# Empty slots in the side stream of a spectral and MLP kernel, row blocks loaded in two halves, and the filter gradient reordered on ScalarE

## The chip, the cores and the metric

The kernel runs on one core of a Trainium2 chip. The metric is the device time of one execution in microseconds (us). TensorE is called PE here, VectorE DVE, ScalarE ACT, GpSimdE POOL and SyncE SP. DMAs are issued from the queues of SP, POOL and, for one kind of load, ACT.

## The reference

The reference is the forward pass and all gradients of a gated mixture of two branches on an input x of 2048 x 1024 (bfloat16):

```
g = sigmoid(sum(x * gate_w))                      # one gate for each row
a = irfft2(rfft2(x) * (w_r + i w_i))              # spectral filter, w of 2048 x 513
h = relu(x @ w1 + b1) ** 2                        # 2048 x 3584
b = h @ w2 + b2
out = g * a + (1 - g) * b
```

Given grad_out, it returns out (out_0) and the gradients of x (out_1), w_r and w_i (out_2 and out_3), w1 (out_4), b1 (out_5), w2 (out_6), b2 (out_7) and gate_w (out_8).

## The kernel before

The program is unrolled completely. Its large products (five times 896 matmuls of 128x512, and a last one that is cut into fewer products) are the main stream of PE. The two-dimensional transforms of x and of the gradient are a side stream of small matmuls that is strewn among them. Both are Python generators: a `yield` is the end of a unit of work, and `spread` (a few lines above the program's end) takes from the side generator as many units as are due after each unit of the main one. A unit with nothing in it, a bare `yield`, is an empty slot.

A planner of the framework fixes the order of each engine's instructions when the program is built. It goes through a simulated time, and gives an engine that is free the instruction that comes first in program order among those that it holds to be ready by then. Program order thus decides only where several instructions are ready. An engine with nothing else to do takes work from far ahead: four loads of w2 (L554) that stand behind the first eight tiles of a stage are issued together at its start. At run time each engine and each DMA queue keeps its fixed order, and where the planner was too hopeful the engine waits, with all that is queued behind.

The stages in order:

- Up to about 446 us: `mlp_in` makes h and its gradient dh for all of the 3584 hidden columns (L667 and L677), stores both (h2T_scr, dhT_scr), and the first half of the transforms of x and grad_out (row tiles, columns) lies among them and goes to z_scr.
- 446 to about 890 us: `mlp_grads` makes the gradients of w2 (L808) and w1 (L824). A main unit is 16 matmuls of 128x512 into one PSUM bank (pw, two banks in turn), which ACT copies out (wo, L812 and L829); there are 112 of them. The side stream is `spectra`, which is `fft_mid` and then `fft_out`. Two main units run first. Then `todo / 110` side units are due after each main unit, with `todo = 3 + 6 * 16 + 2 * 16 = 131`, the number of side units that are to be done by the end.
- 890 to about 1101 us: `mlp_out` makes the forward output (L896) with w2 in SBUF and row blocks of h2T_scr (tile hblk, `blocks.one`, L844: 3584 rows by 256 columns, 1792 KB, two buffers). The second half of `fft_out` lies among it.
- From 1101 us on: `GradOfX` makes the gradient of x from row blocks of dhT_scr (hblk again) and the transposed w1, with a scheme of seven products on quarters of the block: a11 and a21 are the columns 0 to 127 and 128 to 255 of the first half of the 28 row chunks, a12 and a22 those of the second half. DVE makes the sums of quarters (dS L984, dT L991) and adds the products (L1005), in an order that the program chains by hand (`dve`).

The side stream in more detail. `fft_mid` loads am and bm (L308, L310), the first z and wn (L316, L320), and in `edges` the first column of all z (ed, low, mid, L341 to L343), from which PE makes 32 small products (sp, L354). Then, for m from 0 to 15, six units: `transform` twice (px L375, copied to x by ACT, L377), the first product of the inverse of m - 1 (`back`, pv L411), `products` (t, L383 and L385, on DVE) with the second one, `joined` (y, L392 and L393), and a unit with `grads_of_w` and `mirrored` for the next m (pm, L368 and L369, which the next transform reads). The end of `back` makes two tiny products (si, L424) and stores to y_scr (L435). In m = 0 there is no `back`, so it has four units.

`grads_of_w` (L441 to L453) multiplies on DVE into g1 and g2, adds in two pieces for each of the two gradients into gs with the 512 columns written in another order (L446, with the last column in L447), scales by a constant into gw (L449), scales the first and last column once more from gs (L450) and stores gw with four DMAs of POOL's queue.

`fft_out` loads ki and ci, and two row tiles r of y_scr (L505, ACT's queue), which need all that `fft_mid` stored there. Then it has two units for each of 32 tiles: `rows_back` (pki L521, from r and the folded rf, L513 and L514) and `columns_back` (pui L294, folds on DVE, a store to ax_scr).

Of the kernel before, what the change touches and what calls it, by code (L numbers as in the profile page):

```python
# [10 lines left out]
P = 128  # L11
# [3 lines left out]
ALU = mybir.AluOpType  # L15
ACT = mybir.ActivationFunctionType

FDT = FP16
# [3 lines left out]
def pair_of(m, R1):  # L22
    return (m, R1 - m) if m else (0, R1 // 2)
# [112 lines left out]
def kernel(  # L136
# [22 lines left out]
    nc = tc.nc  # L159
# [6 lines left out]
    g = Geo(S, D, F)  # L166
    S2, DC, FC = g.S2, g.DC, g.FC
    R1, R2 = g.R1, g.R2
    NT = S // P
    Q, H, LW, W1 = D // 4, D // 2, g.Df + 1, g.Df  # L170
# [4 lines left out]
    GS = 2.0 / (S * D * XS * XS)  # L175
    SBUF, PSUM, DRAM = bass.MemoryType.SB, bass.MemoryType.PSUM, bass.MemoryType.DRAM
    turned = lambda out, in_: nc.sync.dma_start(out=out, in_=in_, transpose=True)
    ld, st = nc.sync.dma_start, nc.gpsimd.dma_start
    V, mm = nc.vector.tensor_tensor, nc.tensor.matmul
# [10 lines left out]
    def pool(name, side="left", space=SBUF, stack=None, bufs=1):  # L190
        stack = ExitStack() if stack is None else stack
        kw = {} if space == DRAM else dict(side=side, reuse_waits="tile")
        return stack.enter_context(tc.tile_pool(name=name, bufs=bufs, space=space, **kw)), stack

    pers, _ = pool("pers", stack=ctx)
    dram, _ = pool("dram", space=DRAM, stack=ctx)
# [25 lines left out]
    def after(ins, earlier, wait=mybir.DependencyClass.Sync):  # L222

        if earlier is not None:
            info = mybir.DependencyInfo(wait, mybir.DependencyReason.DATA)
            tc.add_manual_dep(ins.ins, earlier.ins.name, info, reason="paced")
# [75 lines left out]
    def fft_mid():  # L302
        fb, fbs = pool("f2", "right")
# [8 lines left out]
        def inputs(m):  # L312
            z = fb.tile([P, 2, 2, H], FDT, name="z", tag="z", bufs=2)
            for n, c in enumerate((m, R1 // 2 + m)):
                for x in range(2):
                    ld(out=z[lanes[x], n], in_=z_scr[:][c, :, x ^ n if m else x])  # L316
            wn = fb.tile([P, 2, LW], BF16, name="wn", tag="wn", bufs=2)
            for c_, src_w in enumerate((A_w_r, A_w_i)):
                for n, k in enumerate(pair_of(m, R1)):
                    ld(out=wn[lanes[n], c_, 0:W1], in_=every(src_w, k))  # L320
            return z, wn
# [50 lines left out]
        def transform(m, n, pm, x):  # L372
            px = fps.tile([P, 2, H], FP32, name="px", tag="ps2", bufs=2)
            for T in range(2):
                mm(px[:, T, :], lhsT=am[:, m, n, :], rhs=pm[:, n, T, :], start=True, stop=True)  # L375
            for c in range(2):
                nc.scalar.copy(out=x[lanes[n], c, :, 0:H], in_=px[lanes[c]])  # L377

        def products(x, w):
            t1_ = fb.tile([P, 2, 2, LW], FDT, name="t1", tag="t1")  # L380
            t2_ = fb.tile([P, 2, 2, LW], FDT, name="t2", tag="t2")
            xw = lambda t: t[:].rearrange("p c t l -> p (c t) l")[:, :, 0:W1]
            V(out=xw(t1_), in0=xw(x), in1=w[:, 0:1, 0:W1].to_broadcast([P, 4, W1]), op=ALU.mult)  # L383
            wi = w[:, 1:3, 0:W1].rearrange("p (o t) l -> p o t l", o=1).to_broadcast([P, 2, 2, W1])
            V(out=t2_[:, :, :, 0:W1], in0=x[:, :, :, 0:W1], in1=wi, op=ALU.mult)  # L385
            return t1_, t2_
# [47 lines left out]
                for h in range(2):  # L434
                    st(out=y_scr[:][c, :, h ^ n if m else h], in_=pc[lanes[h], n])  # L435

        def grads_of_w(m, x):
            XA, XB = (x[:, :, T, 0:W1] for T in range(2))
            t1_ = fb.tile([P, 2, LW], FDT, name="g1", tag="g1")
            t2_ = fb.tile([P, 2, LW], FDT, name="g2", tag="g2")  # L440
            V(out=t1_[:, :, 0:W1], in0=XB, in1=XA, op=ALU.mult)  # L441
            V(out=t2_[:, :, 0:W1], in0=XB, in1=XA[:, ::-1, :], op=ALU.mult)
            gs = fb.tile([P, 2, LW], FDT, name="gs", tag="gs")
            for c, (a, b, op) in enumerate(((t1_[:, 0], t1_[:, 1], ALU.add), (t2_[:, 1], t2_[:, 0], ALU.subtract))):
                grouped = lambda t: t[:, 0:H].rearrange("p (g i) -> p g i", g=4)
                V(out=gs[:, c, 0:H].rearrange("p (i g) -> p g i", g=4), in0=grouped(a), in1=grouped(b), op=op)  # L446
                V(out=gs[:, c, H:W1], in0=a[:, H:W1], in1=b[:, H:W1], op=op)  # L447
            gw = fb.tile([P, 2, LW], BF16, name="gw", tag="gw")
            nc.vector.tensor_scalar(out=gw[:, :, 0:W1], in0=gs[:, :, 0:W1], scalar1=GS, scalar2=None, op0=ALU.mult)  # L449
            nc.vector.tensor_scalar(out=gw[:, :, 0::H], in0=gs[:, :, 0::H], scalar1=0.5 * GS, scalar2=None, op0=ALU.mult)  # L450
            for c_, dst_w in enumerate((out_2, out_3)):
                for n, k in enumerate(pair_of(m, R1)):
                    st(out=every(dst_w, k), in_=gw[lanes[n], c_, 0:W1])  # L453
# [2 lines left out]
        ex = edges()  # L456
        pm, w = mirrored(0, nxt[0]), by_groups(nxt[1])
        nxt = inputs(1)
        held = None
        yield  # L460
        for m in range(NM + 1):
            if m < NM:
                x = fb.tile([P, 2, 2, LW], FDT, name="x", tag="x", bufs=2)
                for n in range(2):
                    transform(m, n, pm, x)
                    yield
                nc.vector.tensor_copy(out=x[:, :, :, 0::H], in_=ex[:, m])
            if held:
                backs = back(m - 1, *held)
                next(backs)  # L470
                yield
            if m < NM:
                ts = products(x, w)
            if held:
                next(backs)
                yield
                for _ in backs:
                    pass
            if m < NM:
                held = joined(m, *ts)  # L480
                yield
                grads_of_w(m, x)
                if m + 1 < NM:
                    pm, w = mirrored(m + 1, nxt[0]), by_groups(nxt[1])
                if m + 2 < NM:
                    nxt = inputs(m + 2)
                yield
        fbs.close()

    def fft_out():  # L490
# [3 lines left out]
        fb, fbs = pool("f3", "right")  # L494
# [59 lines left out]
                    ld(out=w2[:, fc : fc + 4, :], in_=B_w2[fc * P : (fc + 4) * P, :].rearrange("(q p) e -> p q e", p=P))  # L554

        load(0), load(1)
        yield
        yield
        folded(0)
        for n in range(len(tiles) + 1):  # L560
            if n < len(tiles):
# [275 lines left out]
    BW = 2 * P  # L837

    def blocks(scr):
        v_ = scr[:].rearrange("c p s -> p c s")  # L840

        def one(k, earlier=None):
            t_ = later["strm"].tile([P, FC, BW], BF16, name="hblk", tag="strm", bufs=2)
            after(ld(out=t_[:], in_=v_[:, :, k * BW : (k + 1) * BW]), earlier)  # L844
            return t_

        return one
# [326 lines left out]
    for k in range(NT // 4):  # L1174
        i = 4 * k
# [38 lines left out]
    n = 0  # L1214
# [22 lines left out]
    def spectra():  # L1237
        yield from fft_mid()
        yield from fft_out()

    spec, grads = spectra(), mlp_grads()
    next(grads), next(grads)
    todo = 3 + 6 * (R1 // 2) + 2 * NT
    for _ in spread(grads, spec, todo / (2.0 * FG * FGC * NH - 2)):
        pass
    tps_s.close()
    out_, n = mlp_out(), 0
# [44 lines left out]
```

## Time and profile before

| what | before |
|---|---|
| median of 3 runs | 1285.03 us (1284.2 to 1285.09) |
| the profiled execution | 1284.05 us, span 1282.3 us |
| mean granted clock of PE | 0.995 |
| PE busy | 1259.7 us |
| DVE, ACT, POOL busy | 737.9, 474.1, 275.7 us |
| gs adds, L446 and L447 | 32 x 1304 ns and 32 x 277 ns (DVE) |
| gw scaling, L449 and L450 | 16 x 429 ns and 16 x 237 ns (DVE) |
| row blocks hblk | 16 loads of 1792 KB, 8.1 to 10.6 us to landing |
| r from y_scr | 32 loads of 256 KB, 2.7 to 9.7 us to landing, median 4.9 |

How to read it: the span is the time from the first to the last instruction of one profiled execution. Busy times of engines overlap. A group's line gives the source line, the engine, the operation, what it writes and reads, the count, and then the total and the mean of one. A wait names the instruction that waited and the one that released it. A granted clock below 1.00 means that PE ran slower than it can in that stretch: at 0.50 a matmul of 128x512 takes twice as long.

### The profile page before, as it was taken

Reading aid. Unit: us, or ns where it says so; the run is one execution under the profiler, and the core shown is the slowest. Engines: PE = TensorE matmul, PEld = TensorE weight load, DVE = VectorE, ACT = ScalarE, POOL = GpSimd, SP = SyncE. Lnnn points to the kernel's source line nnn. Section 1 sums busy time; section 2 is a strip of 40 time slices with the busy share of each in tenths; the row PEclk is TensorE's granted clock in tenths of the full one; section 3 lists DMA queues with packets and bytes.
Section 4 is the critical chain, followed back from the end, with each engine's and each line's share of the span. In section 5 each row is a group of like instructions: output and inputs, shape, how many; then the busy total and the mean of one; then the engine's idle time right before and its main releaser. Section 6 shows DMA issues by size and latency. Waiting matters only on the chain.

```text
span 1282.3 us, 18371 instructions
## 1 busy us (share of the span) xinstructions
PE 1259.7 (98%) x6884; PEld 610.6 (48%) x6884; DVE 737.9 (58%) x1634; ACT 474.1 (37%) x777; POOL 275.7 (22%) x424
## 2 busy tenths in 40 slices
PE   9999999999999999999999999999999999999997
PEld 5555544555544444444444444555455454444443
DVE  3554433544482237687787772343867767886573
ACT  4656654666633324434433432443112111011100
POOL 0111111111100135445465542222010101000000
PEclk9999999999999999999999999999999999999999
DMA  9566353546344678998879669965899897565530
GB/s 290 201 181 181 132 156 124 180 149 189 107 133 119 149 196 222 237 254 186 197 181 182 165 141 289 272 194 170 223 231 220 192 208 206 163 183 162 166 114 33
DMA packets 326004, 233.27 MB, mean 182 GB/s; under 512 B 195052, under 2 KB 279178, under 8 KB 325658
## 3 DMA queue, kind: packets, MB, share of 16 engines
q1 hardware_dynamic: 290864, 141.19, 46.4%
q0 software_dynamic: 26144, 82.47, 18.9%
q10 hardware_dynamic: 8906, 8.43, 2.3%
q8 instruction: 54, 0.88, 0.3%
q14 instruction: 36, 0.29, 0.1%
HBM read 106.19 MB, written 81.81 MB: 147 GB/s over the span
## 4 chain that ended last, share of the span: by engine, by line
PE 57%; DVE 4%; issue 1%; DMA 0%; ACT 0%; ACTq 0%; DVEq 0%
PE pw L824 15%; PE acc L896 14%; PE pw L808 13%; PE xX L996 7%; PE xV L996 4%; PE xZ L996 1%; PE pui L294 1%; PE pki L521 1%; PE pv L411 1%; PE px L375 1%; DVE dT L991 1%; DMA r<-y_scr 0%; DVE dS L984 0%; DVE af L876 0%; DVE g L963 0%
## 5 line engine op out<-in xcount | busy, mean ns | idle before, releaser
L667 PE MATMUL ph<-xT,w1g 128*128 128x512 bf16 x896 | 221.1, 379 | 1.0 <-DMA w1g<-in_B_w_dram 1.0
L677 PE MATMUL pd<-dbT,w2T 128*128 128x512 bf16 x896 | 211.3, 379 | 0.4 <-DVE dhT L681 0.4
L824 PE MATMUL pw<-grp,res 128*128 128x512 bf16 x896 | 203.2, 381 | 0.0
L808 PE MATMUL pw<-dbn,grp 128*128 128x512 bf16 x896 | 203.0, 383 | 0.0
L896 PE MATMUL acc<-w,hblk 128*128 128x512 bf16 x896 | 198.7, 379 | 0.0
L681 DVE SCALAR_TENSOR_TENSOR dhT<-pd,rT 128x512 bf16<-128x512 f32 x112 | 77.4, 691 | 203.0 <-PE pd L677 162.9
L808 PEld LDWEIGHTS <-grp 128*128 128x128 bf16 x896 | 87.4, 99 | 105.9 <-issue 4.8
L677 PEld LDWEIGHTS <-w2T 128*128 128x128 bf16 x896 | 87.1, 98 | 103.4 <-issue 1.2
L824 PEld LDWEIGHTS <-res 128*128 128x128 bf16 x896 | 86.5, 98 | 99.5 <-issue 2.3
L896 PEld LDWEIGHTS <-hblk 128*128 128x128 bf16 x896 | 86.2, 98 | 98.0
L667 PEld LDWEIGHTS <-w1g 128*128 128x128 bf16 x896 | 84.6, 98 | 90.2 <-DMA w1g<-in_B_w_dram 1.3
L669 ACT ACTIVATE rT<-ph,b1col 128x512 bf16<-128x512 f32 x112 | 77.0, 687 | 115.7 <-PE ph L667 115.7
L829 ACT CAST wo<-pw 128x512 bf16<-128x512 f32 x56 | 32.8, 585 | 131.2 <-PE pw L824 74.1
L812 ACT CAST wo<-pw 128x512 bf16<-128x512 f32 x56 | 32.8, 585 | 128.4 <-PE pw L808 87.9
L962 ACT ACTIVATE g<-gatew_bc,dsc 128x1024 f32<-128x1024 bf16 x16 | 18.3, 1148 | 149.3 <-DVE gxo L1005 123.0
L670 ACT ACTIVATE h2T<-rT 128x512 bf16<-128x512 bf16 x112 | 70.6, 630 | 2.5
L996 PEld LDWEIGHTS <-dS 128*128 128x128 f16 x448 | 43.8, 98 | 52.9
L523 ACT CAST rt<-pki 128x1024 f16<-128x1024 f32 x32 | 32.5, 1016 | 96.4 <-PE pki L521 92.9
L377 ACT CAST x<-px 64x1024 f16<-64x1024 f32 x64 | 64.4, 1007 | 6.9 <-PE px L375 6.2
L283 POOL DMA_DIRECT2D z_scr<-u x32 | 22.7, 710 | 171.6 <-ACT u L278 101.7
L722 POOL DMA_DIRECT2D h2T_scr<-h2T x28 | 19.9, 711 | 183.1 <-ACT h2T L670 167.4
L897 DVE SCALAR_TENSOR_TENSOR ot<-acc,omg,af 128x512 bf16<-128x512 f32 x32 | 24.0, 748 | 52.0 <-PE acc L896 51.9
(188 smaller groups left out, 1613.2 us busy)
## 6 DMA issues: line engine op xcount, KB each, us to landing
h2T_scr<-h2T POOLq DMA_DIRECT2D x28, 512.0 KB, 4.2
dhT_scr<-dhT POOLq DMA_DIRECT2D x28, 512.0 KB, 4.6
hblk<-h2T_scr SPq DMA_DIRECT2D x8, 1792.0 KB, 9.9
hblk<-dhT_scr SPq DMA_DIRECT2D x8, 1792.0 KB, 9.3
z_scr<-u POOLq DMA_DIRECT2D x32, 256.0 KB, 3.0
z<-z_scr SPq DMA_DIRECT2D x64, 128.0 KB, 3.6
y_scr<-pc POOLq DMA_DIRECT2D x64, 128.0 KB, 3.8
r<-y_scr ACTq DMA_DIRECT2D x32, 256.0 KB, 4.9
```

What stands on the lines that cost most here:

```text
L377: nc.scalar.copy(out=x[lanes[n], c, :, 0:H], in_=px[lanes[c]])
L667: mm(ph[:], lhsT=w1g[:, dc, fc % 2 * P : (fc % 2 + 1) * P], rhs=xT[:, dc, ss], start=(dc == 0), stop=(dc == DC - 1))
L669: nc.scalar.activation(rT[:], ph[:], ACT.Relu, bias=b1col[:, fc : fc + 1])
L670: nc.scalar.activation(h2T, rT[:], ACT.Square)
L677: mm(pd[:], lhsT=w_[:, ec, fc % FGC * P : (fc % FGC + 1) * P], rhs=dbT[:, ec, ss], start=(ec == 0), stop=(ec == DC - 1),)
L681: return STT(out=dhT, in0=pd[:], scalar=2.0, in1=rT[:], op0=ALU.mult, op1=ALU.mult, accum_out=gb1part[:, fc, sb : sb + 1],)
L808: mm(pw[:], lhsT=cur[:, t, fb_ * P : (fb_ + 1) * P], rhs=dbn[:, t, hf * H : (hf + 1) * H], start=(t == 0), stop=(t == NT - 1),)
L812: last = nc.scalar.copy(out=wo[:, hf * H : (hf + 1) * H], in_=pw[:])
L824: mm(pw[:], lhsT=xr[t][:, d_ * P : (d_ + 1) * P], rhs=cur[:, t, :], start=(t == 0), stop=(t == NT - 1),)
L829: nc.scalar.copy(out=wo[:], in_=pw[:])
L896: turn["PE"] = mm(acc[:], lhsT=cur[:, fc, t2 * P : (t2 + 1) * P], rhs=w2[:, fc, cs], start=(fc == 0), stop=(fc == FC - 1))
L996: mm(acc[:], lhsT=lhs[:, fc, :], rhs=rhs[:, fc, :], start=start and fc == 0, stop=fc == KH - 1, skip_group_check=True,)
```

## The change

- `fft_mid` gives three slots instead of one after its loads and edge products, and three instead of one at the end of m = 0.
- `fft_out` gives four empty slots instead of two after its first loads.
- `todo` is 137 instead of 131, so the six slots are counted: the side stream stands at the same place when `mlp_grads` ends.
- `grads_of_w` adds without reordering, in one piece for each gradient (513 columns), into gs, which has two buffers now. A new function, `grads_out`, scales and reorders with one multiply of ACT, scales the first and last column on DVE from gs as before, and issues the four stores. It stands behind the first transform of the next m, and for the last m behind the end of `back`.
- Every row block hblk is loaded with two DMAs of 14 row chunks each, for both uses (h2T_scr and dhT_scr).

```diff
-        def grads_of_w(m, x):
+        def grads_of_w(x):
...
-            gs = fb.tile([P, 2, LW], FDT, name="gs", tag="gs")
-            for c, (a, b, op) in enumerate(((t1_[:, 0], t1_[:, 1], ALU.add), (t2_[:, 1], t2_[:, 0], ALU.subtract))):
-                grouped = lambda t: t[:, 0:H].rearrange("p (g i) -> p g i", g=4)
-                V(out=gs[:, c, 0:H].rearrange("p (i g) -> p g i", g=4), in0=grouped(a), in1=grouped(b), op=op)
-                V(out=gs[:, c, H:W1], in0=a[:, H:W1], in1=b[:, H:W1], op=op)
+            gs = fb.tile([P, 2, LW], FDT, name="gs", tag="gs", bufs=2)
+            V(out=gs[:, 0, 0:W1], in0=t1_[:, 0, 0:W1], in1=t1_[:, 1, 0:W1], op=ALU.add)
+            V(out=gs[:, 1, 0:W1], in0=t2_[:, 1, 0:W1], in1=t2_[:, 0, 0:W1], op=ALU.subtract)
+            return gs
+
+        def grads_out(m, gs):
             gw = fb.tile([P, 2, LW], BF16, name="gw", tag="gw")
-            nc.vector.tensor_scalar(out=gw[:, :, 0:W1], in0=gs[:, :, 0:W1], scalar1=GS, scalar2=None, op0=ALU.mult)
+            nc.scalar.mul(
+                out=gw[:, :, 0:H].rearrange("p c (i g) -> p c i g", g=4),
+                in_=gs[:, :, 0:H].rearrange("p c (g i) -> p c i g", g=4), mul=GS,
+            )
             nc.vector.tensor_scalar(out=gw[:, :, 0::H], in0=gs[:, :, 0::H], scalar1=0.5 * GS, scalar2=None, op0=ALU.mult)
             for c_, dst_w in enumerate((out_2, out_3)):
                 for n, k in enumerate(pair_of(m, R1)):
...
-        held = None
-        yield
+        held = gs = None
+        for _ in range(3):
+            yield
         for m in range(NM + 1):
             if m < NM:
                 x = fb.tile([P, 2, 2, LW], FDT, name="x", tag="x", bufs=2)
                 for n in range(2):
                     transform(m, n, pm, x)
                     yield
+                    if n == 0 and gs:
+                        grads_out(m - 1, gs)
...
-                grads_of_w(m, x)
+                gs = grads_of_w(x)
...
-                yield
+                for _ in range(1 if m else 3):
+                    yield
+            else:
+                grads_out(m - 1, gs)
         fbs.close()
...
         load(0), load(1)
-        yield
-        yield
+        for _ in range(4):
+            yield
...
-            after(ld(out=t_[:], in_=v_[:, :, k * BW : (k + 1) * BW]), earlier)
+            for h in range(2):
+                c_ = slice(h * FC // 2, (h + 1) * FC // 2)
+                after(ld(out=t_[:, c_, :], in_=v_[:, c_, k * BW : (k + 1) * BW]), earlier)
...
-    todo = 3 + 6 * (R1 // 2) + 2 * NT
+    todo = 9 + 6 * (R1 // 2) + 2 * NT
```

## The prediction

> **What bounds the kernel now.** I read the page's busy shares first. TensorE (PE) is busy 98% of a 1282.3 us span, VectorE (DVE) 58%, ScalarE (ACT) 37%. PE's work is not changed here, so the change can be worth no more than PE's idle time and the time that PE spends at a lower clock. The second view was therefore the waits of PE, then PE's own order of time around each wait. Of 1282.3 - 1259.7 = 22.6 us of idle time, about 2.7 lie at the very start and 7.3 behind the last matmul; the rest is mostly these lines (engine, line, what it waited for: us in total, times, longest).
>
> ```profile
> PE 1259.7 (98%) x6884; PEld 610.6 (48%) x6884; DVE 737.9 (58%) x1634; ACT 474.1 (37%) x777; POOL 275.7 (22%) x424
> ```
> ```profile
> PE xX L996 <- DMA hblk<-dhT_scr: 2.9, 1, 2.9
> PE pki L521 <- DMA r<-y_scr: 2.9, 1, 2.9
> PE px L375 <- DVE pm L368: 2.4, 1, 2.4
> PE sp L354 <- DVE ed L350: 1.7, 1, 1.7
> ```
> In order of time (start, duration, idle time before in brackets), the beginning of the side stream and the place where its last stage begins:
> ```profile
> 446.31 13.11 PE L808 MATMUL pw<-dbn,grp 128*128 128x512 bf16 x60
> 461.20 5.78 PE L808 MATMUL pw<-dbn,grp 128*128 128x512 bf16 x26
> 468.72 0.16 PE L354 MATMUL sp<-ed,am 128*128 128x4 f16 x1 [1.74 <-DVE ed L350]
> 469.95 10.70 PE L808 MATMUL pw<-dbn,grp 128*128 128x512 bf16 x41
> 483.05 0.60 PE L375 MATMUL px<-pm,am 128*128 128x512 f16 x2 [2.40 <-DVE pm L368]
> ...
> 773.85 7.07 PE L824 MATMUL pw<-grp,res 128*128 128x512 bf16 x32
> 783.82 0.40 PE L521 MATMUL pki<-ki,r 128*128 128x128 f16 x4 [2.90 <-DMA r<-y_scr]
> ```
> The reader is to see that each wait stands in front of the first side-stream matmul of a stage, and that main-stream matmuls, which need nothing, are queued behind it. There is a second cost, in the table by stretches (length, busy times, then the granted clock after POOL):
> ```profile
> 470.00:472.00 2.00, 2.00 (x11) 0.81 (x9) 1.65 (x6) 0.58 (x1) 0.32 (x1) 0.66 0.58 128
> 472.00:474.00 2.00, 2.00 (x7) 0.63 (x5) 2.00 (x4) 0.00 (x0) 1.14 (x2) 0.50 0.78 215
> ...
> 484.00:486.00 2.00, 2.00 (x7) 0.78 (x7) 1.21 (x3) 1.96 (x3) 1.68 (x4) 0.57 1.17 221
> 486.00:488.00 2.00, 2.00 (x7) 0.69 (x5) 0.20 (x1) 1.96 (x3) 1.90 (x3) 0.58 1.18 282
> ...
> 784.00:786.00 2.00, 2.00 (x12) 0.87 (x10) 0.29 (x2) 1.01 (x1) 0.54 (x1) 0.66 1.00 357
> 786.00:788.00 2.00, 2.00 (x6) 0.76 (x5) 0.49 (x2) 0.00 (x0) 0.00 (x0) 0.50 1.06 388
> ```
> After each of the three waits the clock is lowered for some 4 us. Missing clock times length gives the loss: (0.34 + 0.50) x 2 = 1.7 us each. So the wait at px costs 2.40 + 1.7 = 4.1 us and the one at pki 2.90 + 1.7 = 4.6 us. Between 500 and 775 us PE is busy 275.00 of 275.00 us: nothing is to be had there.
>
> **The change, part by part.**
>
> *Two more empty slots before the first transform and two after it.* They issue nothing; they only place what follows later in program order. Slots are handed out per main unit of 16 matmuls (16 x 0.2157 = 3.45 us), starting with the third unit: 131/110 = 1.191 slots per unit before, 137/110 = 1.245 after. Before, the transform of m = 1 is slot 6, due after unit 7, at 112 matmuls; the trace has it behind 60+5+26+2+41 = 134, so the planner thought it ready only then, and was 2.4 us of idle and 1.7 us of slow clock too hopeful. After, it is slot 10: 1.245 x 8 = 9.96, so after unit 10, at 160 matmuls. Is pm there by then? The transforms of m = 0 move to 80 and 96 matmuls; from PE's rows the second is at about 471 us. Then come two copies (ACT L377, 1.0 each), the edge column (0.18), t 1.23, g 0.69 twice, t 1.2 to 2.1, gs 0.42 twice, y 0.7 four times, ye 0.5, pm 0.7: ready at about 483.5. PE reaches 160 matmuls at 470 + 65 x 0.2157 + 0.4 + 1.7 (slow clock after sp) = 486. So pm is some 2.5 us early and the 4.1 us go.
>
> The sp wait stays: its 32 small matmuls hang on the edge loads and DVE copies of slot 1, which no slot moves; PE arrives at the same time whether it has done px before or not. I take 0; its ends are -3.4 (wait and slow clock both go) and +1.7 (a longer wait).
>
> *Two more empty slots before the first row tile of the last stage.* Before, the last si is in slot 98 (unit 82 counted from the third) and the first pki in slot 100 (unit 84): 32 matmuls between, as the trace shows. After, slots 102 and 106 fall on units 82 and 85: 48 matmuls, 10.35 us. The data needs 783.82 - 773.85 = 9.97 us (y_scr stores, then r, issued at 778.18 beside four loads of w2). So r is about 0.4 us early and 4.6 us go; the r landings in this trace run from 2.7 to 9.7 us, median 4.9, so a rest of 0 to 1 us may stay. What is late next is r of the next tile, needed one unit later (about 788.7 against 786.7): not late.
>
> The slot rate rises by 4.6%. Per transform step PE is then at 18.3 us instead of 19.05; in the trace DVE has pm done 14 us and y 6 us before PE asks, so I cost it at nothing. If this cover were gone, a stall of 0.2 us in each of 16 steps would be 3 us.
>
> *The filter gradient.* DVE loses 2 x 1.304 (L446, strided writes) + 2 x 0.277 (L447) + 0.429 (L449) and gains 2 adds of 513 elements, 0.42 each by L543: 3.59 - 0.84 = 2.75 us per step, 44 us in all (if the odd width made them as slow as L446, 1.0). ACT gains one multiply of 1024 elements: between 1.007 (L377) and 1.148 (L962, also SBUF to SBUF); I take 1.1, 17.6 us in all. Neither engine ends a wait of PE between 500 and 775, where DVE is busy 203 and ACT 111 of 275 us: 0. The Trainium skill, page "ScalarE: Activation LUTs", section "Rules for kernel authors", speaks against this edit: it says to put multiplications on VectorE. By its formula for an ACTIVATE with immediate operands, 186 + 0.833 x 1024 = 1039 ns, against 0.43 for L449 in this trace; by the rule 16 x 0.6 = 10 us would be lost if ACT set the pace, by PE's row nothing.
>
> The new wait: ACT's multiply waits for gs, and queued behind it on ACT are the copies wo of the main stream and x of the transforms; DVE's two-column fix-up now waits for ACT, with pc and y queued behind; POOL's four gw stores (0.53 each) wait for that, with wo and y_scr stores and w copies behind. POOL already waits 40.2 us in 15 steps for gw. A wo copy has about 2.9 us before PE needs its bank (ACT idles 2.87 before it). That covers the multiply and 1.8 us of lateness. The second gs buffer keeps the next sum from waiting.
>
> *Row blocks in halves.* SP issues 16 more loads, 16 x 0.38 = 6 us, with the a_, go, gx and xo loads behind them; the blocks of the forward product land some 20 us early. The one block that PE waits for is the second dhT block (2.90 us, at 1110.05). Its first half is all that the first product reads, and would land near 1106.6 by halving what 8.9 us is above the 2 to 3 us of the smallest loads: so this wait goes. But time does not:
> ```profile
> 1095.10:1126.20 31.10, 27.35 (x127) 12.18 (x126) 31.03 (x28) 1.15 (x1) 0.54 (x1) 1.00 0.43 127
> ```
> DVE is busy 31.03 of 31.10 us here, in a fixed order, up to the add that frees the bank for the product at 1126.18. PE would stand before the second dT (about 1.2 us) and before that add (2.5 us) instead: the same 3.75 us. I take 0; the ends are -0.5 and +1.7, since the new wait of 2.5 us may bring a slow clock, which the present one of 2.90 did not. On the clock the Trainium skill, "TensorE: Matmul & The Clock Gate", section "Part 1: The HAM clock gate", says that the clock falls after an idle window of about 3.4 us. By it, none of these waits would cost clock and the gain would be 5.3 us. The trace differs, with slow stretches after 1.74, 2.40 and 2.90 us, and it decides.
>
> *Sum:* 2.40 + 1.7 + 2.90 + 1.7 = 8.7 us. The profiled execution took 1284.05 (its span and 1.75 around it), so 1275.3 for it; the median of the runs shown is 1285.03, 0.98 above, so the forecast is 1276.3.
>
> **The rivals.** *One of the two gains fails* (pm or r still late, r being the likelier with its 0.4 us of margin): -4.1 to -4.6, and 1280.6. For it speaks that the planner was wrong by 4 us at px; against it, that strided gs, 1.7 us of that chain, is gone. *Both gains, but a slow stretch elsewhere* (the new wait before 1126): 1278.0. *Nothing changes:* the planner may hold the stage's first matmul where it was; program order binds only where PE has other ready work. Against it: si to pki is 32 matmuls, exactly two units. About 1285. *Slower: ACT is held up by gs.* If DVE runs later than planned by L, the wo copy behind the multiply is late by up to L + 1.1 - 2.9 us, and PE stalls, in those of the 16 steps where the multiply stands just ahead of wo. At L = 4.1 (the error at px) this is about 2/3 of the steps at 1.1 us, with 12 us lost against 8.7 gained: 1288. It decides from L of about 3.7. For it: the gw stores near 761 were placed ahead of a wo that was ready 1.2 us before them, so L is about 2 there. Against: most of that L is the strided gs that goes.
>
> **How the numbers follow.** Chances: forecast 0.54, one gain 0.18, both with a slow stretch 0.08, nothing 0.06, slower 0.14. A measurement of this kernel tells differences over about 0.2%, 2.6 us; faster are the first three, 0.80. The forecast's own range is 1274.5 to 1278.5 (r late by up to 1 us, the sp wait by a little). The low end is 1273.0: the sp wait and its slow stretch go too (-3.4). The high end, 1283.0, takes in the case of one gain with a slow stretch of 1.7, and leaves out nothing-changes and slower, 0.20.
>
> **What would show it.** In the profile after, the lines px from pm and pki from r are gone from PE's waits, and the clock of 0.50 after them too; PE has 160 and 48 main matmuls where it had 134 and 32; sp still waits about 1.7. xX no longer waits for hblk but about 3.7 us for DVE before 1126. DVE is down by about 44 us, ACT up by about 18. The prediction is wrong if PE waits for pw's banks (ACT wo late behind the multiply), or if pki still waits for r by more than 1 us.

## The result, and the profile after

The changed kernel takes 1280.97 us (median of 4 runs, 1279.91 to 1281.83) where the kernel before took 1284.97: 4.0 us less, a ratio of 0.997 with a 95% interval of 0.9952 to 0.9987. The forecast was 8.7 us less, 1276.3. The time lies in the range of the prediction (1273.0 to 1283.0) and on the side that it gave 0.80, but less than half of the gain is there. The profiled execution took 1281.81 us, with a span of 1280.0 and a mean granted clock of 0.997.

The busy times first. Columns are engine, busy us, share of the span and instructions. Some of PE's matmuls are missing from this record (6753 of 6884), so its busy time is not compared.

```profile
PE 1249.9 (98%) x6753; PEld 609.6 (48%) x6884; DVE 705.3 (55%) x1586; ACT 503.0 (39%) x793; POOL 275.3 (22%) x424
```

DVE has 32.6 us less to do, ACT 28.9 more. The second view is again the waits of PE (us in total, times, longest):

```profile
PE pw L818 <- ACT wo L822: 4.9, 3, 2.7
PE xX L1008 <- DVE g L1017: 2.3, 2, 1.2
PE sp L354 <- DVE ed L350: 1.7, 1, 1.7
PE pw L834 <- ACT wo L839: 1.7, 2, 0.8
...
PE xX L1008 <- DVE dT L1003: 1.1, 1, 1.1
```

The waits at px, at pki and for hblk, which headed this list before, are gone. At the head stands one that was not there: the main stream's matmuls wait for ACT to copy their PSUM bank out (wo). PE's own order of time shows both (start, duration, idle time before in brackets):

```profile
470.26 13.98 PE L818 MATMUL pw<-dbn,grp 128*128 128x512 bf16 x62
484.07 0.59 PE L375 MATMUL px<-pm,am 128*128 128x512 f16 x2
485.69 3.61 PE L818 MATMUL pw<-dbn,grp 128*128 128x512 bf16 x16 [1.02 <-ACT wo L822]
...
497.40 7.07 PE L818 MATMUL pw<-dbn,grp 128*128 128x512 bf16 x31
504.30 1.03 PE L375 MATMUL px<-pm,am 128*128 128x512 f16 x4
508.05 5.30 PE L818 MATMUL pw<-dbn,grp 128*128 128x512 bf16 x16 [2.73 <-ACT wo L822]
...
583.63 3.61 PE L818 MATMUL pw<-dbn,grp 128*128 128x512 bf16 x15 [1.17 <-ACT wo L822]
...
676.39 3.61 PE L834 MATMUL pw<-grp,res 128*128 128x512 bf16 x16 [0.83 <-ACT wo L839]
...
696.42 3.61 PE L834 MATMUL pw<-grp,res 128*128 128x512 bf16 x16 [0.82 <-ACT wo L839]
...
776.49 0.19 PE L424 MATMUL si<-ye,bm 128*128 128x4 f16 x2
776.54 10.52 PE L834 MATMUL pw<-grp,res 128*128 128x512 bf16 x47
786.90 0.39 PE L531 MATMUL pki<-ki,r 128*128 128x128 f16 x4
```

px at 484.07 and pki at 786.90 have no bracket: nothing was waited for. The five waits for wo are 1.02 + 2.73 + 1.17 + 0.83 + 0.82 = 6.57 us, four of them in the stretch from 500 to 775, where in the kernel before PE was busy without a gap. The order of ACT around the longest of them says why (same columns):

```profile
497.59 0.58 ACT L822 CAST wo<-pw 128x512 bf16<-128x512 f32 x1 [2.43 <-issue]
505.61 1.92 ACT L450 ACTIVATE gw<-gs 128x1024 bf16<-128x1024 f16 x1 [7.43 <-DVE gs L445]
507.44 1.05 ACT L822 CAST wo<-pw 128x512 bf16<-128x512 f32 x2
```

The bank that PE wants back at 505.32 was full at about 500.9 (the 16 matmuls from 497.40 on, 0.216 each), and ACT was idle. But the multiply stands ahead of the copy in ACT's fixed order and waits until 505.61 for the sums gs. The copy begins at 507.44, 6.5 us after it could have. It would have been done 3.8 us before PE asked for the bank (505.32 - 501.5); 6.5 - 3.8 is the wait of 2.7. And DVE has the sums late because its own order holds something else in front (the order of DVE, same columns):

```profile
495.15 0.69 DVE L368 TENSOR_TENSOR pm<-z 128x1024 f16<-128x1024 f16 x1 [9.77 <-DMA z<-z_scr]
```

This pm is the one of m = 3 (the third pm in DVE's order), and the products and sums of m = 1 stand behind it. Its z is no later than it was: the last loads are issued from 487.96 us on, before from 488.95. But in the kernel before, the sums of m = 1 stood ahead of the pm of m = 3, and when DVE came to this pm, z was there (the kernel before, same columns):

```profile
497.83 0.21 DVE L447 TENSOR_TENSOR gs<-g 128x1 f16<-128x1 f16 x1
497.88 0.68 DVE L368 TENSOR_TENSOR pm<-z 128x1024 f16<-128x1024 f16 x1
```

The planner has turned the two round.

The granted clock, in stretches of 2 us (length, busy times, then the clock after POOL's):

```profile
486.00:488.00 2.00, 2.00 (x11) 0.88 (x10) 0.00 (x0) 1.99 (x3) 2.00 (x5) 1.00 1.34 230
...
508.00:510.00 2.00, 1.95 (x6) 0.79 (x6) 1.06 (x2) 1.99 (x4) 1.97 (x4) 0.62 0.32 66
510.00:512.00 2.00, 2.00 (x6) 0.71 (x5) 0.00 (x0) 1.96 (x3) 0.65 (x2) 0.53 0.91 215
...
786.00:788.00 2.00, 1.95 (x16) 1.14 (x16) 0.49 (x2) 0.80 (x2) 0.00 (x0) 1.00 0.88 193
```

The slow stretches after px and pki are gone (1.00 at 486 and at 786), and by the same view the one after sp too, although sp still waits 1.66 us; a new one stands behind the wait of 2.73 us and costs (0.38 + 0.47) x 2 = 1.7 us. So the account of the span is: gained 4.1 (px) + 4.6 (pki) + 1.7 (the slow clock after sp) + 0.35 (hblk's 3.75 became 3.40) = 10.75; lost 6.57 + 1.7 = 8.3. That leaves 2.45, and the spans differ by 1282.3 - 1280.0 = 2.3. The 1.7 us after sp are hardly the change's doing: sp waits 1.66 us here and waited 1.74 before, and in the kernel with the old gradient (below), where it waits 1.73, the slow clock is there again (0.57 and 0.58 from 470 to 474 us).

### The profile page after: what moved, and what is told of

It is laid out like the page before. It is cut to its first block, busy times and chain, and to the rows that moved or that the text cites. A ratio compares the mean times of both kernels' runs of the same rounds, so it can differ in the third digit from the quotient of the medians.

```text
span 1280.0 us, 18253 instructions
## 1 busy us (share of the span) xinstructions
PE 1249.9 (98%) x6753; PEld 609.6 (48%) x6884; DVE 705.3 (55%) x1586; ACT 503.0 (39%) x793; POOL 275.3 (22%) x424
## 5 line engine op out<-in xcount | busy, mean ns | idle before, releaser
L677 PE MATMUL ph<-xT,w1g 128*128 128x512 bf16 x864 | 216.9, 379 | 2.7 <-DMA w1g<-in_B_w_dram 1.1
L818 PE MATMUL pw<-dbn,grp 128*128 128x512 bf16 x876 | 200.2, 381 | 5.8 <-ACT wo L822 4.9
L834 PE MATMUL pw<-grp,res 128*128 128x512 bf16 x872 | 198.8, 379 | 2.9 <-ACT wo L839 1.7
L377 ACT CAST x<-px 64x1024 f16<-64x1024 f32 x64 | 64.4, 1007 | 0.7
L450 ACT ACTIVATE gw<-gs 128x1024 bf16<-128x1024 f16 x16 | 31.6, 1972 | 57.3 <-DVE gs L445 52.2
```

Source lines behind the costliest of these rows:

```text
L677: mm(ph[:], lhsT=w1g[:, dc, fc % 2 * P : (fc % 2 + 1) * P], rhs=xT[:, dc, ss], start=(dc == 0), stop=(dc == DC - 1))
L818: mm(pw[:], lhsT=cur[:, t, fb_ * P : (fb_ + 1) * P], rhs=dbn[:, t, hf * H : (hf + 1) * H], start=(t == 0), stop=(t == NT - 1),)
L834: mm(pw[:], lhsT=xr[t][:, d_ * P : (d_ + 1) * P], rhs=cur[:, t, :], start=(t == 0), stop=(t == NT - 1),)
```

## The experiments

The theory after this reading: the slots are worth what was forecast, and the multiply on ACT gives half of it back. Rivals: the multiply is simply too long (1.97 us each, 1.1 forecast); its place in ACT's order does it, whatever its length; the sums are late because of DVE's order; or the slots themselves are worth less. All are kernels built from the two shown, and the ratios are to the kernel before, run on the same chip. The last column is the median of the kernel before in the same set of runs. The changed kernel was timed in a set of its own, so a row is compared with it by gains or ratios; differences of 1 us between medians of two sets say nothing.

| kernel | us (range) | ratio, 95% interval | before |
|---|---|---|---|
| changed | 1280.97 (1279.91 to 1281.83) | 0.997, 0.9952 to 0.9987 | 1284.97 |
| slots and halves, gradient as before | 1277.01 (1276.88 to 1279.6) | 0.9945, 0.993 to 0.996 | 1285.08 |
| gradient alone | 1287.58 (1285.27 to 1291.24) | 1.0018, 1.0008 to 1.0028 | 1285.08 |
| halves alone | 1285.65 (1282.92 to 1288.56) | 1.0008, 0.9997 to 1.0019 | 1285.08 |
| fft_mid's slots alone | 1286.56 (1281.76 to 1289.54) | 1.0003, 0.9988 to 1.0018 | 1285.76 |
| fft_out's slots alone | 1281.77 (1281.01 to 1284.0) | 0.997, 0.996 to 0.9981 | 1285.76 |
| changed, strided write | 1285.88 (1282.21 to 1288.02) | 1.0002, 0.999 to 1.0014 | 1285.08 |
| changed, contiguous multiply | 1287.34 (1285.44 to 1288.74) | 1.0017, 1.0007 to 1.0027 | 1285.15 |
| changed, multiply behind the x copies | 1274.86 (1273.34 to 1278.4) | 0.9915, 0.989 to 0.994 | 1285.15 |
| changed, multiply on DVE | 1277.09 (1275.57 to 1278.01) | 0.9935, 0.9914 to 0.9956 | 1285.15 |
| changed, gs ahead of pm | 1279.43 (1278.41 to 1280.54) | 0.9948, 0.9933 to 0.9962 | 1285.76 |
| old gradient, edge products later | 1272.97 (1271.8 to 1273.24) | 0.9902, 0.9882 to 0.9922 | 1285.15 |
| both orders | 1272.09 (1271.62 to 1273.38) | 0.9892, 0.9877 to 0.9907 | 1285.76 |

**Parts alone: the changed kernel with the old gradient.** From the changed kernel (the single buffer of gs and the place of the stores go back too):

```diff
-            V(out=gs[:, 0, 0:W1], in0=t1_[:, 0, 0:W1], in1=t1_[:, 1, 0:W1], op=ALU.add)
...
+                V(out=gs[:, c, 0:H].rearrange("p (i g) -> p g i", g=4), in0=grouped(a), in1=grouped(b), op=op)
...
-            nc.scalar.mul(
...
+            nc.vector.tensor_scalar(out=gw[:, :, 0:W1], in0=gs[:, :, 0:W1], scalar1=GS, scalar2=None, op0=ALU.mult)
```

> Empty slots and halves as in the changed kernel, the filter gradient as before (summed, reordered and scaled on DVE). Theory 1 (ACT's multiply stands ahead of the wo copies in ACT's order and waits there for gs): PE's waits for wo, 6.6 us in the changed kernel, are gone and so is the slow clock behind the one of 2.73 us; px, sp and pki cost what they cost in the changed kernel; 1273 to 1277 us. Theory 2 (the denser side stream and the shifted loads make the waits, whoever scales the gradient): PE waits for wo or for pv and px some 4 us or more, 1279 to 1282 us.

It took 8.1 us less than before. PE's waits have no wo; there is one new wait, at the fifth tile of fft_out (807.07 us):

```profile
PE pki L523 <- ACT rt L525: 2.7, 1, 2.7
...
PE sp L354 <- DVE ed L350: 1.7, 1, 1.7
```

So slots and halves bring about the gain that the prediction gave to the whole change, and the new gradient costs some 4 us of it (a gain of 8.1 against 4.0; the two intervals just overlap). That is less than the 8.3 us of waits and slow clock in the account above, because this kernel has losses of its own in their place: in the profiled run, the slowest of its four (1279.6; the others, without a profile, took 1276.88 to 1277.04), the wait of 2.7 us at pki and slow clocks of 1.7 us after it and after sp.

**The new gradient alone**, on the kernel before:

```diff
-            nc.vector.tensor_scalar(out=gw[:, :, 0:W1], in0=gs[:, :, 0:W1], scalar1=GS, scalar2=None, op0=ALU.mult)
+            nc.scalar.mul(
+                out=gw[:, :, 0:H].rearrange("p c (i g) -> p c i g", g=4),
+                in_=gs[:, :, 0:H].rearrange("p c (g i) -> p c i g", g=4), mul=GS,
+            )
```

> The kernel before with the new filter gradient only (multiply on ACT, gs in two buffers), no added slots, whole row blocks. Theory 1: PE waits for wo by 3 to 8 us in several steps, and the three waits of the kernel before stay; 1287 to 1294 us. Theory 2: no wait for wo; the time is that of before, 1283 to 1286 us, or a little less where the shorter DVE chain brings pm earlier (px waits 0 to 2.4 us).

It is 2.5 us slower than before (1.0018, interval above 1). Its profiled execution, the slowest of the ten (1291.24 us):

```profile
PE pki L529 <- DMA r<-y_scr: 3.6, 1, 3.6
PE pw L816 <- ACT wo L820: 3.4, 4, 0.9
...
PE px L375 <- DVE pm L368: 1.5, 1, 1.5
...
PE pv L411 <- ACT x L377: 1.1, 2, 1.0
```

Waits for wo come without any new slot, and the inverse's first product (pv) now waits for ACT's x copies too. The 41 us that the groups of gs and gw take less on DVE show up in PE's waits nowhere but at px (2.4 to 1.5).

**The halves alone:**

```diff
-            after(ld(out=t_[:], in_=v_[:, :, k * BW : (k + 1) * BW]), earlier)
+            for h in range(2):
+                c_ = slice(h * FC // 2, (h + 1) * FC // 2)
+                after(ld(out=t_[:, c_, :], in_=v_[:, c_, k * BW : (k + 1) * BW]), earlier)
```

> The kernel before with row blocks in halves only. My prediction: the wait of xX for hblk (2.90) goes and waits for dT and for the adds of 3.4 to 3.8 us in all take its place, since DVE is busy without a pause there; 1284 to 1286 us. Rival: PE starts the next products earlier for good, 1281 to 1282.5 us.

No difference beyond the interval. The wait for hblk has become three waits for the DVE chain, as the prediction said:

```profile
PE xX L998 <- DVE g L1007: 2.3, 2, 1.2
...
PE xX L998 <- DVE dT L993: 1.0, 1, 1.0
```

**Each pair of slots alone.** On the kernel before, first only those around the first transforms, then only those of fft_out:

```diff
-        yield
+        for _ in range(3):
+            yield
...
-    todo = 3 + 6 * (R1 // 2) + 2 * NT
+    todo = 7 + 6 * (R1 // 2) + 2 * NT
```

> Kernel before with only the four slots around the first transforms (todo 135), nothing else. Theory of the prediction's sum: the wait at px (2.40 us) and its slow clock (1.7 us) go, the one at pki (2.9 us and 1.7 us) stays: 1285.0 - 4.1 = 1280.9. Rival (a stall that is taken away comes back as another one of the same stage, as the wait at pki did as 2.7 us with both sets of slots): no more than 1 us is gained.

```diff
-        yield
-        yield
+        for _ in range(4):
+            yield
         folded(0)
...
-    todo = 3 + 6 * (R1 // 2) + 2 * NT
+    todo = 5 + 6 * (R1 // 2) + 2 * NT
```

> Kernel before with only the two slots ahead of the first row tile (todo 133), nothing else. Theory of the prediction's sum: the wait at pki goes with its slow clock, the one at px stays: 1285.0 - 4.6 = 1280.4. Rival: r is still late or ACT is, as in the kernel with both sets of slots and the old gradient, where pki waited 2.7 us for a copy of ACT: 0 to 1 us gained.

The first set gains nothing (1.0003), the second 4.0 us. Waits of PE in the kernel with the first set, and then in the one with the second:

```profile
PE pki L523 <- DMA r<-y_scr: 5.8, 1, 5.8
PE xX L998 <- DVE dT L993: 2.7, 1, 2.7
```
```profile
PE px L375 <- DVE pm L368: 4.1, 1, 4.1
PE xX L996 <- DMA hblk<-dhT_scr: 3.1, 1, 3.1
PE sp L354 <- DVE ed L350: 1.6, 1, 1.6
...
PE pki L521 <- DMA r<-y_scr: 1.2, 1, 1.2
```

With the first set the wait at px is gone, but pki waits 5.8 us instead of 2.9. The last si is at 773.88 as before (773.80), but POOL issues the last store to y_scr at 778.51, where before it was at 775.57, and r is issued behind that store. POOL's order is the same in both (a store to y_scr, one of wo, the last one to y_scr); what held the last store for 2.86 us I did not find, and the trace shows no releaser. It begins 0.89 us after the start of ACT's wo copy at 777.62, as stores of wo do after their copies (0.88), which hints at that copy but does not show it.

So one set alone was not worth its term of the sum: 4.1 us was forecast and nothing measured. For the second set 4.6 was forecast and 4.0 measured, but not by that term alone: 1.2 us of pki's wait is left, px waits 4.1 us instead of 2.4, and in the profiled run sp had no slow clock (1.00 from 468 to 472 us), 1.7 us that these slots have nothing to do with. Together the sets brought 8.1. The terms held for the pair, not for each alone: an edit at one end of the stage changed a wait at the other end, by a way that is only partly known.

**The multiply's form.** In the changed kernel it reads with a stride and writes contiguously. First the other way round:

```diff
             nc.scalar.mul(
-                out=gw[:, :, 0:H].rearrange("p c (i g) -> p c i g", g=4),
-                in_=gs[:, :, 0:H].rearrange("p c (g i) -> p c i g", g=4), mul=GS,
+                out=gw[:, :, 0:H].rearrange("p c (i g) -> p c g i", g=4),
+                in_=gs[:, :, 0:H].rearrange("p c (g i) -> p c g i", g=4), mul=GS,
             )
```

> The changed kernel with ACT's multiply going through the elements in the other order: gs is read contiguously, gw written with a stride. The same values. If the strided read from SBUF makes it 1.97 us: 1.0 to 1.15 us each, the waits of PE for wo shrink by some 0.9 us each, to 2 to 3 us in all, 1276 to 1280 us. If the multiply costs 1.97 us in either order: waits of 6 to 7 us, 1280 to 1282 us.

The expectation that the multiply would be short when it reads contiguously and writes with a stride was wrong. By the trace (min/median/max, ns):

```profile
L450 ACT ACTIVATE gw<-gs x16: 2476/2500/2514, 484.3 to 765.7; 128x1024 bf16<-128x1024 f16 x16
```

It is 0.53 us longer, the waits for wo are 8.0 us instead of 6.6, and the gain of the whole change is gone (1.0002). Not all of that is the multiply's: in the profiled run sp waited 2.27 us and had its slow clock of 1.7 us, which the profile of the changed kernel did not have. Then with no stride at all on ACT (DVE writes the sums in the other order, as in the kernel before):

```diff
-            V(out=gs[:, 0, 0:W1], in0=t1_[:, 0, 0:W1], in1=t1_[:, 1, 0:W1], op=ALU.add)
...
+                V(out=gs[:, c, 0:H].rearrange("p (i g) -> p g i", g=4), in0=grouped(a), in1=grouped(b), op=op)
...
+            nc.scalar.mul(out=gw[:, :, 0:W1], in_=gs[:, :, 0:W1], mul=GS)
```

> The changed kernel, but DVE reorders in its adds as before, so that ACT's multiply reads and writes contiguously. The multiply: 1.0 to 1.15 us instead of 1.97. If its length makes PE wait, PE's waits for wo fall from 6.6 to 2 to 3 us and the time to about 1277 us. If its place does (ACT stands and waits for gs, with wo behind), gs comes some 1.8 us later still and the waits stay at 5 us or more, 1280 to 1283 us.

The multiply is short now, about as long as the prediction took it, and the kernel is 2.2 us slower than before:

```profile
L452 ACT ACTIVATE gw<-gs x16: 1060/1061/1062, 487.1 to 767.6; 128x1026 bf16<-128x1026 f16 x16
```
```profile
PE pw L817 <- ACT wo L821: 6.7, 7, 2.4
...
PE pw L833 <- ACT wo L838: 1.3, 2, 1.0
```

8.0 us of waits for wo, with a multiply of half the length: ACT's waits for gs grew from 52.2 us in 14 steps to 73.4 in 16, and the strided sums make gs later. So the length of the multiply does not explain the waits: with half of it they are longer in all. How late gs is, with wo behind it, does, and in this place the length comes on top (0.53 us more of it went with 1.4 us more of waiting, above).

**The multiply's place.** The same multiply, ordered behind the x copies of the first transform of the next pair of rows (an order on ACT without a semaphore):

```diff
-                nc.scalar.copy(out=x[lanes[n], c, :, 0:H], in_=px[lanes[c]])
+                last_x[0] = nc.scalar.copy(out=x[lanes[n], c, :, 0:H], in_=px[lanes[c]])
...
-            nc.scalar.mul(
+            scaled = nc.scalar.mul(
...
+            after(scaled, last_x[0], mybir.DependencyClass.NoSync)
```

> The changed kernel, with the multiply of 1.97 us kept in ACT's order behind the two x copies of the first transform of the next m (an order on ACT alone, no semaphore), so that gs is there when ACT comes to it. If the wait for gs is what costs: ACT's waits for gs fall from 52 us to under 10, PE's waits for wo to under 1.5, 1275.5 to 1278.5 us, as with the old gradient. If the length of 1.97 us costs by itself: PE still waits for wo by 3 us or more, 1279 us or more.

This is 10.3 us faster than before, with an interval of the ratio (0.989 to 0.994) clear of the changed kernel's, and no wait for wo is left in the profile:

```profile
L450 ACT ACTIVATE gw<-gs 128x1024 bf16<-128x1024 f16 x16 | 31.4, 1963 | 2.4 <-DVE gs L445 2.4
```
```profile
PE sp L354 <- DVE ed L350: 2.6, 1, 2.6
...
PE pki L533 <- ACT rt L535: 1.7, 1, 1.7
```

The first line has the multiply at 1963 ns as ever, with 2.4 us of waiting for gs in the whole run where it had 52.2. So the later place costs PE nothing that shows, and ACT does carry 31 us of extra work for nothing. Moved to DVE instead, where the multiply also goes through the elements in the other order, as in the strided write above:

```diff
-            nc.scalar.mul(
-                out=gw[:, :, 0:H].rearrange("p c (i g) -> p c i g", g=4),
-                in_=gs[:, :, 0:H].rearrange("p c (g i) -> p c i g", g=4), mul=GS,
...
+            nc.vector.tensor_scalar(
+                out=gw[:, :, 0:H].rearrange("p c (i g) -> p c g i", g=4),
+                in0=gs[:, :, 0:H].rearrange("p c (g i) -> p c g i", g=4), scalar1=GS, scalar2=None, op0=ALU.mult,
```

> The changed kernel with the reordering multiply on DVE in place of ACT; all else the same. PE's waits for wo are gone; DVE has slack in every step (203 of 275 us busy before). 1275.5 to 1278.5 us. If the two-buffer gs and the place of grads_out matter and not ACT: 1280 us or more.

1277.09: no waits for wo either, and the same gain as with the old gradient (8.1 us). This kernel keeps the two buffers of gs and the place of `grads_out`, so these are not what costs. The multiply takes 1.33 us there:

```profile
L450 DVE TENSOR_SCALAR gw<-gs x16: 1319/1330/2119, 488.2 to 757.2; 128x1024 bf16<-128x1024 f16 x16
```

**Where the lateness comes from.** On DVE, pm is put behind the sums that come before it in program order, so that waiting for z no longer holds gs:

```diff
-            V(out=pm[:, 0], in0=z[:, 0], in1=z[:, 1], op=ALU.add)
+            first = V(out=pm[:, 0], in0=z[:, 0], in1=z[:, 1], op=ALU.add)
+            after(first, last_gs[0], mybir.DependencyClass.NoSync)
...
-            V(out=gs[:, 1, 0:W1], in0=t2_[:, 1, 0:W1], in1=t2_[:, 0, 0:W1], op=ALU.subtract)
+            last_gs[0] = V(out=gs[:, 1, 0:W1], in0=t2_[:, 1, 0:W1], in1=t2_[:, 0, 0:W1], op=ALU.subtract)
```

> The changed kernel with one order more on DVE: pm of the next pair of rows stands behind the gradient sums gs of the one before it. In the changed kernel pm waits 9.8 us for z at 495, with the sums of m = 1 queued behind; the multiply waits for them, and a wo copy behind the multiply keeps PE waiting for 2.7 us, with 1.7 us of slow clock after it. Theory (this DVE wait makes the multiply late): the wait of 2.7 us at 508 is gone, with its slow clock, and the other four waits for wo (1.02, 1.17, 0.83 and 0.82) stay or shrink: 1281.0 - 4.4 = 1276.6, or down to 1272.7 if these go too. Rival (the multiply's fixed place ahead of wo does it, wherever DVE stands): waits for wo of together 5 us or more remain, and the time is within 1 us of 1281.

The wait at 508 is gone with its slow clock, as expected. The other four are there, now of 0.40 and three of 0.87, together 3.0 us:

```profile
487.35 3.61 PE L820 MATMUL pw<-dbn,grp 128*128 128x512 bf16 x16 [0.40 <-ACT wo L824]
...
580.41 3.61 PE L820 MATMUL pw<-dbn,grp 128*128 128x512 bf16 x16 [0.87 <-ACT wo L824]
...
673.22 3.61 PE L836 MATMUL pw<-grp,res 128*128 128x512 bf16 x16 [0.87 <-ACT wo L841]
...
693.29 3.61 PE L836 MATMUL pw<-grp,res 128*128 128x512 bf16 x16 [0.87 <-ACT wo L841]
```

It gains 6.3 us on the kernel before, where the changed kernel gained 4.0: 2.3 us more, and 4.4 were expected; the intervals of the two ratios overlap. In the profiled run the span is 3.0 us shorter (1277.0 against 1280.0), although sp waited 2.38 us and had its slow clock again, 0.7 + 1.7 us more than in the changed kernel's profile.

So pm ahead of the sums explains the longest of the five waits. The other four do not hang on it. In the changed kernel no wait for z stands ahead of them: before the one at 583.63 DVE works without a pause from 571.36 to 581.12 us, with the pc adds (L418 and L419, 1.2 us each) and y in front of the sums, and ACT waits 5.46 us for these sums. Among the kernels tried the four go only where the multiply is moved behind the x copies or off ACT.

**What beats both kernels.** The wait at sp is the last large one. The 32 edge products are moved behind the second transform of m = 0, first with the old gradient, then with the multiply behind the x copies:

```diff
-        ex = edges()
+        ed = edges()
...
+                if m == 0:
+                    ex = edge_products(ed)
                 nc.vector.tensor_copy(out=x[:, :, :, 0::H], in_=ex[:, m])
```

> Empty slots and halves, the old gradient on DVE, and the 32 edge products (sp) moved in program order behind the second transform of m = 0 (112 main matmuls instead of some 93). By the order of PE in the changed kernel the edge data is there at 468.4 us and PE comes to it at about 471: the sp wait of 1.7 us and its slow clock of 0 to 1.7 us go, and pm is not later since x is what it waits for. 1.7 to 3.4 us less than with the old gradient alone: 1273 to 1275.5 us. Rival: the DVE chain from ex on is late and px waits for pm instead, 1277 us or more.

> The changed kernel with two orders more: the multiply behind the x copies of the next pair of rows, and the 32 edge products (sp) behind the second transform of m = 0. Theory (the two losses are separate: a wait for the edges ahead of the transforms, and wo copies queued behind the multiply): no wait at sp, none for wo; 1274.9 minus the 2.6 us that PE waited at sp with the multiply moved alone, so 1272.3, and down to 1270.6 if a slow stretch of 1.7 us hung on that wait. Rival (the old gradient on DVE is the better one, since the multiply still takes 31 us of ACT): a wait for wo comes back, and the time is above the 1273.0 of the old gradient with the edges moved.

1272.97 and 1272.09: 1.0 and 1.1% faster than before, and not to be told apart. In neither does sp wait. With both orders, the largest that are left:

```profile
PE xX L1015 <- DVE g L1024: 2.3, 2, 1.2
PE pki L538 <- ACT rt L540: 1.4, 1, 1.4
```

## Why the prediction was right in part

- *The extra slots take away the waits at px and pki, 8.7 us: right,* with luck in it. Both waits and both slow stretches are gone, and with the old gradient the measured gain is 8.1. px and pki have 156 (79 + 12 + 2 + 1 + 62) and 47 recorded main matmuls in front of them, where 160 and 48 were said. But pm did not come 2.5 us early behind the whole chain of m = 0, as the prediction had it: the planner put this pm ahead of the products of m = 0 (470.75 to 473.45 us), and px came at 484.07. Where an order holds the half of pm that the first px reads behind the sums of m = 0 (gs ahead of pm), it is done at 485.38 and px comes at 486.35: the path that was described suffices, with 1.0 us to spare. At pki, r was there by 786.24, 0.66 us early (0.4 were said); with fft_out's slots alone it was 1.17 us late. And the two terms are not separate: alone, the first set brought 0 and the second 4.0.
- *sp keeps its wait: right* (1.66 us). Its slow clock went in the profiled execution, which the low end had held open; in most of the other kernels it is there.
- *Halves at nothing: right,* and by the way described: hblk's 3.75 us became 1.05 + 1.13 + 1.22 = 3.40 before the DVE chain, and halves alone measured 1.0008, with 1 inside the interval.
- *The filter gradient at nothing: wrong, and this is the step that failed.* The sentence was that neither engine ends a wait of PE between 500 and 775. This held for the kernel before; it says that neither had work enough to be late, not that nothing of theirs could be placed so as to be late. The prediction named the mechanism and its cover ("A wo copy has about 2.9 us before PE needs its bank ... That covers the multiply and 1.8 us of lateness") and then used it as an exclusive rival at 0.14 instead of as a term of the sum. What the runs showed is between: 5 waits in 16 steps, 6.6 us, and 1.7 us of slow clock, beside the gains and not in their place; with only the multiply's place changed, all five are gone and the gain is 10.3 us. The rival's price does not follow from its formula either: at L = 4.1 it gives up to 2.3 us for a step, where 1.1 was taken. The case against the rival was that the strided sums, most of the old lateness, go. They went (0.42 and 0.57 us on average now), but the sums were late for other reasons: for the longest wait a pm that waits for z and was placed ahead of them on DVE, for the others the work that DVE has in front of them. With the new gradient alone, where no slot moved anything, no wait for wo is above 0.9 us (four waits, 3.4 us).
- *One of the two gains fails, 1280.6:* the measured 1280.97 lies beside this rival's number by chance. Both gains came, and a loss that the sum did not have took half of it back.
- *The multiply at 1.1 us: mis-sized.* It takes 1.97. The rows that it was taken from (L377, L962) were contiguous ones; with a contiguous read it is indeed 1.06. The experiments say that the extra 0.9 us, by itself, cost nothing once the place was right.
- *DVE down by 44 us, ACT up by 18:* the gs and gw groups fell by 41.0 (49.0 + 10.7 to 15.9 + 2.8, durations that overlap in part), DVE as a whole by 32.6; ACT rose by 28.9. None of these numbers set the time.

On the rule of the Trainium skill, "ScalarE: Activation LUTs", section "Rules for kernel authors", that multiplications belong on VectorE: the runs agree with it for this kernel as changed (a gain of 4.0 us on ACT, 8.1 on DVE), though not for its reason, the time of one element. The multiply is shorter on DVE (1.33 us, against 2.50 on ACT in the same order and 1.97 in the changed kernel's), but with the multiply in a place where it need not wait, ACT does it for nothing (a gain of 10.3 us).

## What to carry to other kernels

Work moved to an idle engine is not free because that engine is idle: look at what stands behind it in the engine's fixed order, and ask when its input is there. An instruction that may wait long is to stand behind the copies that free the bottleneck's buffers, or behind something that itself shows its input is ready; its length matters less than its place. When an edit lets a planner order a stage anew, gains that were read off separate waits need not hold one by one, and a term for new waits belongs into the sum.

## What the runs showed of the hardware

- The price of a 16-bit reorder on ACT, SBUF to SBUF, 1024 elements: 1.06 us contiguous (1026 elements), 1.97 read with a stride and written contiguously, 2.50 read contiguously and written with a stride. On DVE the last of these orders is 1.33. The Trainium skill, "ScalarE: Activation LUTs", section "What ACT_TABLE_LOAD costs", gives 186 ns + 0.833 ns per element for a scale and a bias in the instruction, so by estimate 1.04 us for 1024; the contiguous one agrees, the others are 1.9 and 2.4 times that.
- The time lost to the slow clock came in pieces of 1.7 us, 3.4 us at half speed: none, one or two per wait, and not by the length of the wait alone. One piece came with waits of 1.73 us (sp, old gradient), 1.74 (sp, before), 2.40 and 2.90 (px and pki, before) and 2.98 (hblk, gradient alone); none with 1.56 and 1.66 (sp, fft_out's slots alone and the changed kernel), 1.73 (wo at 700 us, strided write), 2.32 (wo at 638 us, contiguous multiply), 2.74 (dT, fft_mid's slots alone), 2.90 (hblk, before) and 3.10 (hblk, fft_out's slots alone). With the waits of 3.64 and 5.79 us at pki (gradient alone, fft_mid's slots alone) and the one of 4.05 us at px (fft_out's slots alone) there were two in a row, here the last:

```profile
480.00:482.00 2.00, 0.00 (x0) 0.00 (x0) 1.97 (x7) 0.00 (x0) 0.04 (x1) 0.80 1.10 303
482.00:484.00 2.00, 1.28 (x4) 0.46 (x5) 2.00 (x7) 0.21 (x1) 0.01 (x1) 0.50 1.19 224
484.00:486.00 2.00, 2.00 (x6) 0.73 (x5) 0.88 (x2) 1.97 (x3) 2.00 (x4) 0.50 1.17 255
486.00:488.00 2.00, 2.00 (x6) 0.76 (x5) 0.10 (x1) 1.85 (x2) 1.80 (x3) 0.50 0.89 174
```

(0.20 + 0.50 + 0.50 + 0.50) x 2 = 3.4 us, of which some 0.8 fell into the wait itself, which ended at 482.72, and cost nothing. The Trainium skill, "TensorE: Matmul & The Clock Gate", section "Part 1: The HAM clock gate", has a window of 3413 ns that runs freely, and so is met at any phase. By estimate from it, half speed for one window costs 1.7 us, which agrees with the pieces, and the phase would explain that equal waits differ; this was not tested. Its figure that a whole idle window is needed does not agree: waits of 1.73 to 2.98 us were enough in the five cases above.
